# Attention feeding a top-1 mixture of experts: the threshold's float16 parts subtracted by TensorE in PSUM, and the first expert's low halves subtracted from a PSUM copy

## The chip, the cores and the metric

One Trainium2 chip, one core of it, one launch. The metric is device microseconds of the core, the median of a few executions. The engines of the core are named as the profile names them: PE (TensorE matmuls) and PEld (its weight loads), DVE (VectorE), ACT (ScalarE), POOL (GpSimd), SP (SyncE, which here only issues transfers).

## The reference

Thresholded attention over 8 batches of 8 heads (sequence 576, head dimension 64), then a mixture of 8 experts in which each token goes to one expert:

```python
scores = scale * np.matmul(q, k.transpose(0, 1, 3, 2))
thresh = np.max(scores, axis=-1, keepdims=True) - tau
scores = np.where(scores >= thresh, scores, -1000000000.0)
attn = np.exp(scores - np.max(scores, axis=-1, keepdims=True))
attn = attn / (np.sum(attn, axis=-1, keepdims=True) + 1e-09)
x = np.matmul(attn, v)                  # laid out as 4608 tokens of 512
logits = x @ w_gate                     # 8 experts, expert_idx = argmax
h = np.maximum(xe @ w1[e], 0.0)         # 512 -> 1024, tokens of expert e
out[mask] = gate_w[mask, None] * (h @ w2[e])
```

All matmuls run in float16 with a number split in a high and a low half, `hi = f16(x)` and `lo = f16(x - hi)`, so that three products stand for one in float32.

## The kernel before, in words

The attention works on 32 pairs of heads. A pair takes 11 **steps**; the loop over steps writes out, for each step k, one `st_unit` of pair n (transposed scores less the threshold, exponential, mask), one `s_unit` of a later pair, 21 steps ahead, (plain scores, of which DVE takes the row maxima, L324 and L319), and then the products with v of an earlier pair (`av_piece`, L422 to L424). Side work is posted to a step with `plan(k, ...)` or `after(k, ...)` and comes in one of three places: FRONT, MID (after the two units' matmuls) or END (after the mask, ahead of the products with v). `chain(1, [...])` posts its items half a step apart, beginning at the MID of the next step. A planner then orders each engine's instructions: it takes the written order as priority and works with durations of its own, so an instruction may move past others on its engine. `tc.keep_in_program_order` forbids that one instruction moves ahead of what was written before it on its engine.

**The threshold.** `parts(n)` takes the minimum of the negated row maxima (L331), turns the 9 columns with a TensorE transpose into a bank of PSUM (tile `pst`, L335, out of the pool `ps_m`, which has one bank for `pst`, `lg`, `rk` and `pc`), and cuts `x + thr` into three float16 parts (tile `ptT`): ACT makes the first (L340), DVE forms the rest in PSUM (L341), ACT rounds it (L342), DVE subtracts once more (L343). Three small DMAs on SP then put the parts in rows 64 to 66 of the tile `CQ` (L348), where the `st_unit` of the same pair reads them through L361, about seven steps later.

**Low halves.** `low_part` (L244, L245) is the way in which q, k and v get theirs: TensorE multiplies the high half by a float16 identity into a bank of `ps_sc` (6 banks, shared with the score tiles), and DVE subtracts that bank from the scaled input. The experts' weights get theirs in `split_w`: ACT makes the high half of a 128 x 1024 chunk (L730), and one DVE instruction subtracts it, both tensors in SBUF (L731).

**The first expert's weights.** While the last two pairs run, the eight chunks of expert 0 are loaded through two buffers (`wf`, 512 KB each, L717 on SP) and split, one chunk a step from step 318 on (`WS0` = 6 and `WSD` = 1 from step 312); the load of chunk i + 2 is written at the step of split i and must wait until split i has read its buffer. The experts' matmuls (L819, L852) begin to be mixed in about step 342 and fill TensorE from 640 us to the end. The other experts' weights go through eight buffers.

Of the kernel before, what the change touches and what calls it, by code (L numbers as in the profile page):

```python
# [9 lines left out]
F16 = mybir.dt.float16  # L10
# [3 lines left out]
AF = mybir.ActivationFunctionType  # L14
ALU = mybir.AluOpType
AX = mybir.AxisListType

P = 128
# [21 lines left out]
SW = 64.0  # L40
# [2 lines left out]
CAP = NTOK  # L43

TUNE = dict(
    lead=10, cast=2, sl=8, ll=15, sp0=3, sps=0, lv=-16, sv0=-6, sv1=2, av=2, g=4, l=3, d=4, g5=4, l5=3, d5=2, g6=1, l6=2, d6=2, g7=1, l7=1, d7=1, off=2, off5=1, off6=11, lg=4, lg7=13, km=16, rate=15, dh=1, do=3, ws0=6, wsd=1, w1d=5, plv=1, xv=3, so=0, sto=0, ord=0, sc=6, fa=3, fd=4, wa1=-70, wa2=-86, wl1=-28, wl2=-6, avb=1, route=1, ranks=7, pp=8, ew=4, maskat=0, w1a=-40, w1b=3,
)


# [1 line left out]
def kernel(  # L51
# [9 lines left out]
    nc = tc.nc  # L61

    cpool = ctx.enter_context(tc.tile_pool(name="cpool", bufs=1))
# [7 lines left out]
    ew = ctx.enter_context(tc.tile_pool(name="ew", bufs=4))  # L71
# [8 lines left out]
    pp = apool.enter_context(tc.tile_pool(name="pp", bufs=8))  # L80


    ident = cpool.tile([P, P], F32, name="ident")
    make_identity(nc, ident)
    ident_h = cpool.tile([P, P], F16, name="ident_h")
    nc.gpsimd.tensor_copy(ident_h, ident)
    ones = cpool.tile([P, P], F16, name="ones")
    nc.gpsimd.memset(ones, 1.0)
    before = cpool.tile([P, P], F16, name="before")
# [3 lines left out]
    thr = cpool.tile([P, 1], F32, name="thr")  # L93
# [75 lines left out]
    FRONT, MID, END = range(3)  # L169
# [3 lines left out]
    def plan(k, f, where=END):  # L173
        if urgent[0]:
            f = hurry(f)
        assert (k, where) >= (now[0], slot[0])
        acts.setdefault(k, ([], [], []))[where].append(f)
# [11 lines left out]
    def after(k, f, where=END):  # L189
        plan(now[0] + k, f, where)  # L190

    def chain(k, fs, at_once=False):

        if at_once:
            for f in fs:
                after(k, f, END)
            return
        for i, f in enumerate(fs):
            i += slot[0] > FRONT and k == 0
            after(k + i // 2, f, END if i % 2 else MID)  # L200
# [37 lines left out]
    def low_part(x, hi, lo, scale, nm):  # L238

        sc = ps_sc.tile([P, 512], F32, tag="sc", name=f"hi_{nm}")  # L240
        y = sc[:, 0:hi.shape[1]] if len(hi.shape) == 2 else (
            sc[:, 0:hi.shape[1] * hi.shape[2]].rearrange("p (t d) -> p t d", t=hi.shape[1])
        )
        nc.tensor.matmul(y, ident_h, hi, start=True, stop=True)  # L244
        nc.vector.scalar_tensor_tensor(lo, x, scale, y, ALU.mult, ALU.subtract)  # L245
# [80 lines left out]
    def parts(n):  # L326


        nm = st[n]["nm"]
        r = small.tile([P, 9], F32, tag="r", name=f"r_{n}")  # L330
        nc.vector.tensor_reduce(r, nm.rearrange("p a t -> p t a"), axis=AX.X, op=ALU.min)  # L331

        def turn():
            ps = ps_m.tile([P, 512], F32, tag="m", name=f"pst_{n}")
            nc.tensor.transpose(ps[0:9, 0:P], r, ident)  # L335
            x, y = ps[0:9, 0:P], ps[0:9, P:2 * P]
            t = small.tile([9, 3, P], F16, tag="ptT", name=f"ptT_{n}", bufs=1)
            v, a = nc.vector, nc.scalar
            chain(1, [
                lambda: a.activation(t[:, 0], x, AF.Identity, bias=thr[0:9]),  # L340
                lambda: v.scalar_tensor_tensor(y, x, thr[0:9], t[:, 0], ALU.add, ALU.subtract),  # L341
                lambda: a.copy(t[:, 1], y),  # L342
                lambda: (v.tensor_tensor(t[:, 2], y, t[:, 1], ALU.subtract), rows(t)),  # L343
            ])

        def rows(t):
            for p in range(3):
                nc.sync.dma_start(  # L348
                    st[n]["CQ"][64 + p:65 + p].rearrange("p (t c) -> p t c", t=9), t[:, p]
                )  # L350

        after(1, turn)
# [372 lines left out]
    def split_w(e, w, c):  # L725
        wf = wq.pop((e, w, c))

        o = (wb1, wb2)[w][0 if e == "x" else e % 2][:, c].rearrange("p (a h d) -> p a h d", a=w + 1, h=2)
        x = wf.rearrange("p (a d) -> p a d", a=w + 1)
        nc.scalar.activation(o[:, :, 0], x, AF.Copy, scale=SW)  # L730
        nc.vector.scalar_tensor_tensor(o[:, :, 1], x, SW, o[:, :, 0], ALU.mult, ALU.subtract)  # L731

    def late(m):
# [258 lines left out]
    for i in range(8):  # L992
        plan(k + WS0 + WSD * i, lambda i=i: split_w(*wseq[i]))
        if i + 2 < 8:
            plan(k + WS0 + WSD * i, lambda i=i: load_w(*wseq[i + 2]))
# [31 lines left out]
    for e in range(1, E + NL):  # L1027
        for w in range(2):
            for c in range(4):
                i = 4 * w + c  # L1030
# [26 lines left out]
    def weights(j):  # L1057
        turn[0] = j + 1
        split_done.add(wseq[j])
        split_w(*wseq[j])  # L1060
        if j + 8 < len(wseq):
            load_w(*wseq[j + 8])
# [4 lines left out]
    if True:  # L1067
# [9 lines left out]
        while busy:  # L1077
# [3 lines left out]
            for z in (("st", "s"), ("s", "st"))[TUNE["ord"]]:  # L1081
                n, t = divmod(k + (NSTEP + LEAD if z == "s" else 0), NSTEP)
# [11 lines left out]
            n, t = divmod(k - TUNE["av"], NSTEP)  # L1094
# [25 lines left out]
    with tc.For_i(NL, total) as m:  # L1120
        idx = small.tile([P, 2], I32, tag="idx", name="idx_x", bufs=1)
        nc.vector.tensor_copy(idx.unsqueeze(1), T["row"][:, ds(m, 1)])
        bad = small.tile([P, 2], I32, tag="badx", name="bad_x", bufs=1)
        nc.vector.tensor_copy(bad.unsqueeze(1), T["bad"][:, ds(m, 1)])
        regs["x"] = nc.sync.value_load(T["esi"][0:1, ds(m, 1)], min_val=0, max_val=E - 1)
        for w in range(2):
            for c in range(4):
                load_w("x", w, c)
                split_w("x", w, c)
        slots["x"] = idx, bad, 0  # L1130
        fetch("x")
        for g in gemm1, gemm2:
            for _ in g(("x",)):
                chunk[0] += 1
            while mo:
                for _, f in mo.pop(min(mo)):
                    f()
# [52 lines left out]
```

## Time and profile before

| | before |
|---|---|
| median of 3 runs | 1040.5 us (1040.37 to 1044.72) |
| the profiled execution's own time | 1042.02 us |
| its span, first to last instruction | 1040.3 us |
| mean granted TensorE clock | 0.976 of full speed |
| PE, DVE, ACT, POOL busy | 92%, 69%, 63%, 53% of the span |

The busy shares are means over two unlike halves: the attention, to about 600 us, in which PE, DVE, ACT and POOL are all busy most of the time, and the experts, from 640 us, in which PE alone is. A busy PE is an upper bound of its work, since its pipelined matmuls overlap: two matmuls that start 0.22 us apart each last 0.38 us. In a list of instructions the time from one start to the next is what one costs its engine.

### The profile page before, as it was taken

The page shows a single profiled execution, that of the slowest core. Times are in us where ns is not written, and L with a number is a line of the kernel's source. Part 1 is how long each engine was busy: PE and PEld are TensorE (multiplying, and loading weights), DVE is VectorE, ACT ScalarE, POOL GpSimd, SP SyncE. Part 2 cuts the span into 40 slices and gives each one's busy share as a digit, 9 for nine tenths or more (in the row PEclk, how much of TensorE's full clock was granted, in tenths as well). Part 3 has the DMA queues.
Part 4 walks back from the last instruction along what each step waited for, and adds up shares of the span by engine and source line. Part 5 has one row for each costly group of instructions (what it writes and reads, how often), then busy time and mean ns, then how long its engine had stood idle before and what let it go on. Part 6 is the DMA issues. An engine that isn't in the chain of part 4 may idle for free.

```text
span 1040.3 us, 28272 instructions
## 1 busy us (share of the span) xinstructions
PE 958.2 (92%) x11336; PEld 622.9 (60%) x11336; DVE 719.1 (69%) x1443; ACT 653.1 (63%) x1098; POOL 556.3 (53%) x460
## 2 busy tenths in 40 slices
PE   2799998999898998998996689999999999999996
PEld 1365655566464665564663476767766676667683
DVE  6999998899797997997998964664332433423650
ACT  2588998888787987987977773524342433433641
POOL 3266887976977967968867773153221222122121
PEclk9999999899999999999998898999999999999998
DMA  6534554754465645546534536989746746556720
GB/s 185 140 92 110 138 131 116 164 122 116 132 156 144 134 102 155 139 105 180 127 87 134 140 84 214 310 266 236 231 142 172 232 132 178 170 156 217 225 82 25
DMA packets 142562, 159.16 MB, mean 153 GB/s; under 512 B 96345, under 2 KB 112731, under 8 KB 142428
## 3 DMA queue, kind: packets, MB, share of 16 engines
q1 hardware_dynamic: 126796, 100.35, 37.7%
q10 hardware_dynamic: 6480, 27.53, 8.9%
q0 software_dynamic: 9152, 29.45, 8.7%
q8 instruction: 90, 1.47, 0.6%
q14 instruction: 44, 0.36, 0.1%
HBM read 90.24 MB, written 19.44 MB: 105 GB/s over the span
## 4 chain that ended last, share of the span: by engine, by line
PE 50%; DVE 7%; issue 6%; DMA 4%; ACT 3%; POOL 1%; another core or an unknown queue 1%; POOLq 0%; ACTq 0%; DVEq 0%; SPq 0%
PE h L819 16%; PE y L852 14%; PE st L360 3%; PE s L312 3%; PE s L314 3%; PE st L361 3%; PE av L422 2%; DMA out_dram<-o,gt 2%; DVE wb L731 2%; PE av L423 2%; PE av L424 2%; DVE e L380 2%; DVE nm L324 1%; DMA wf<-in_w_dram 1%
## 5 line engine op out<-in xcount | busy, mean ns | idle before, releaser
L386 POOL TENSOR_TENSOR pl<-e,ph 128x1024 f16<-128x1024 f32 x158 | 336.8, 2142 | 144.2 <-ACT ph L385 103.2
L377 ACT ACTIVATE e<-st,ntau 128x512 f32<-128x512 f32 (+1 forms) x352 | 223.1, 653 | 65.5 <-PE st L361 36.2
L324 DVE TENSOR_REDUCE nm<-s 128x1 f32<-128x512 f32 x320 | 200.4, 633 | 39.9 <-PE s L314 26.0
L380 DVE SCALAR_TENSOR_TENSOR e<-st,e 128x512 f32<-128x512 f32 (+1 forms) x352 | 219.8, 635 | 5.4 <-ACT e L377 4.6
L852 PE MATMUL y<-wb,hl 128*128 128x512 f16 (+1 forms) x1056 | 203.6, 362 | 1.1 <-issue 0.7
L819 PEld LDWEIGHTS <-wb 128*128 128x128 f16 x2304 | 190.4, 99 | 23.3 <-issue 4.9
L819 PE MATMUL h<-xTm,wb 128*128 128x256 f16 (+2 forms) x2112 | 198.0, 255 | 3.1 <-issue 3.1
L422 PE MATMUL av<-vop,ph 128*128 128x65 f16 (+1 forms) x1536 | 186.3, 195 | 4.7 <-issue 2.5
L424 PE MATMUL av<-vop,ph 128*128 128x64 f16 (+1 forms) x1536 | 185.7, 196 | 2.3 <-issue 2.3
L423 PE MATMUL av<-vop,pl 128*128 128x65 f16 (+1 forms) x1536 | 184.8, 194 | 3.2 <-issue 2.9
L385 ACT CAST ph<-e 128x1024 f16<-128x1024 f32 x160 | 166.8, 1043 | 18.6 <-DVE e L380 18.3
L422 PEld LDWEIGHTS <-ph 128*128 128x128 f16 (+1 forms) x1536 | 148.8, 101 | 31.5 <-issue 11.9
L423 PEld LDWEIGHTS <-pl 128*128 128x128 f16 (+1 forms) x1536 | 148.6, 100 | 29.1 <-issue 12.3
L312 PE MATMUL s<-QK 128*128 128x512 f16 (+3 forms) x640 | 141.4, 299 | 24.7 <-DMA QK<-lo 17.3
L424 PEld LDWEIGHTS <-ph 128*128 128x128 f16 (+1 forms) x1536 | 148.7, 100 | 24.7 <-issue 11.5
L731 DVE SCALAR_TENSOR_TENSOR wb<-wf,wb 128x1024 f16<-128x1024 f32 x96 | 125.2, 1341 | 49.1 <-ACT wb L730 45.7
L852 PEld LDWEIGHTS <-hl 128*128 128x128 f16 (+1 forms) x1056 | 94.5, 100 | 101.3 <-issue 6.3
L360 PE MATMUL st<-QK 128*128 128x512 f16 (+3 forms) x640 | 142.4, 298 | 8.8 <-DVE e L380 5.3
L361 PE MATMUL st<-CQ,ck 128*128 128x512 f16 (+3 forms) x640 | 139.7, 293 | 0.7 <-DMA CQ<-hi 0.4
L314 PE MATMUL s<-ck,CQ 128*128 128x512 f16 (+3 forms) x640 | 137.8, 292 | 1.2 <-DMA CQ<-hi 1.2
L864 POOL DMA_INDIRECT out_dram<-o,gt x40 | 44.4, 1111 | 143.9 <-ACT o L863 127.1
L807 ACT ACTIVATE hl<-h 128x512 f16<-128x512 f32 (+1 forms) x80 | 45.8, 573 | 113.6 <-PE h L819 106.7
(182 smaller groups left out, 1092.8 us busy)
## 6 DMA issues: line engine op xcount, KB each, us to landing
wf<-in_w_dram SPq DMA_DIRECT2D x96, 512.0 KB
qkf<-in_qk_dram ACTq DMA_DIRECT2D x30, 576.0 KB
vf<-in_v_dram ACTq DMA_DIRECT2D x15, 640.0 KB
QK<-hi SPq DMA_DIRECT2D x64, 144.0 KB
QK<-hi SPq DMA_DIRECT2D x64, 72.0 KB
QK<-lo SPq DMA_DIRECT2D x64, 72.0 KB
ck<-lo SPq DMA_DIRECT2D x64, 72.0 KB
CQ<-hi SPq DMA_DIRECT2D x64, 64.0 KB
```

What stands on the lines that cost most here:

```text
L312: nc.tensor.matmul(sc[rows, oc], d["QA"][a][:, cols], d["KB"][a][:, CH[c]], start=True, stop=False)
L324: nc.vector.tensor_reduce(o, sc[:, 0:width(t)], axis=AX.X, op=ALU.max, negate=True)
L360: nc.tensor.matmul(sc[rows, oc], d["KB"][a][:, cols], d["QA"][a][:, CH[c]], start=True, stop=False)
L361: nc.tensor.matmul(sc[rows, oc], d["CK"][a][:, cols], d["CQ"][:, q], start=False, stop=True)
L377: nc.scalar.activation(pf, sc, AF.Exp, bias=ntau, scale=0.125 / SS)
L380: nc.vector.scalar_tensor_tensor(pf, sc, 0.0, pf, ALU.is_ge, ALU.mult)
L386: (nc.vector if (n, t) in PLV else nc.gpsimd).tensor_tensor(l, pd, h, ALU.subtract)
L422: nc.tensor.matmul(av, h, vop[:, tv, 0:W], start=i in (0, NT) and m == 0, stop=False)
L423: nc.tensor.matmul(av, l, vop[:, tv, 0:W], start=False, stop=False)
L424: nc.tensor.matmul(av[:, 0:D], h, vop[:, tv, W:W + D], start=False, stop=last)
L819: nc.tensor.matmul(o, Wt[:, c, wh, f], x, start=c == 0 and z == 0, stop=c == 3 and z == 2,)
L852: nc.tensor.matmul(o, h[:, hh], Wt[:, f, wh, c], start=f == 0 and z == 0, stop=f == 7 and z == 2)
```

## The change

Three edits. (1) In `parts`, the two DVE instructions go. ACT makes all three parts with the same instruction, `part(p)`, and between them TensorE subtracts the part just made from the bank, `less(p)`: a matmul of a 9 x 9 matrix of minus one on the diagonal by the 9 x 128 part, added to what the bank holds. The chain has five items in place of four, so the third part and its DMAs are posted half a step later. (2) In `split_w`, for expert 0 alone, the low half is made by `low_part` in two pieces of 512 columns, posted two steps after the high half, one at MID and one at END; the high half is kept in program order on ACT. (3) The splits of expert 0, and the loads that are written with them, are two steps apart (`wsd=2`). One small DVE instruction at the start makes the 9 x 9 matrix.

```diff
-    ... ws0=6, wsd=1, w1d=5 ...
+    ... ws0=6, wsd=2, w1d=5 ...
+    minus = cpool.tile([9, 9], F16, name="minus")
+    nc.vector.tensor_scalar(minus, ident[0:9, 0:9], -1.0, None, ALU.mult)
@@ parts: turn()
-            nc.tensor.transpose(ps[0:9, 0:P], r, ident)
-            x, y = ps[0:9, 0:P], ps[0:9, P:2 * P]
+            nc.tensor.matmul(ps[0:9, 0:P], r, ident, start=True, stop=True, is_transpose=True)
+            x = ps[0:9, 0:P]
             t = small.tile([9, 3, P], F16, tag="ptT", name=f"ptT_{n}", bufs=1)
+            def part(p):
+                nc.scalar.activation(t[:, p], x, AF.Identity, bias=thr[0:9])
+            def less(p):
+                nc.tensor.matmul(x, minus, t[:, p], start=False, stop=True, skip_group_check=True)
             chain(1, [
-                lambda: a.activation(t[:, 0], x, AF.Identity, bias=thr[0:9]),
-                lambda: v.scalar_tensor_tensor(y, x, thr[0:9], t[:, 0], ALU.add, ALU.subtract),
-                lambda: a.copy(t[:, 1], y),
-                lambda: (v.tensor_tensor(t[:, 2], y, t[:, 1], ALU.subtract), rows(t)),
+                lambda: part(0), lambda: less(0), lambda: part(1), lambda: less(1), lambda: (part(2), rows(t)),
             ])
@@ split_w
-        nc.scalar.activation(o[:, :, 0], x, AF.Copy, scale=SW)
+        hi = nc.scalar.activation(o[:, :, 0], x, AF.Copy, scale=SW)
+        if e == 0:
+            tc.keep_in_program_order(hi)
+            for i in range(2):
+                t = slice(512 * i, 512 * i + 512)
+                y = (x[:, i], o[:, i, 0], o[:, i, 1]) if w else (x[:, 0, t], o[:, 0, 0, t], o[:, 0, 1, t])
+                after(2, lambda y=y, i=i: low_part(*y, SW, f"w{w}_{c}_{i}"), END if i else MID)
+            return
         nc.vector.scalar_tensor_tensor(o[:, :, 1], x, SW, o[:, :, 0], ALU.mult, ALU.subtract)
```

## Rows read from the trace of the kernel before

**Rows 1.** Busy time by stretch (from and to in us of the span, its length, then busy us and count of instructions for PE, PEld, DVE, ACT, POOL; then the granted clock, the DMA engines' share, GB/s): the steady attention, the stretch of the eight splits, what follows it, and the experts.

```profile
60.00:540.00 480.00, 457.37 (x6693) 281.06 (x6691) 427.69 (x909) 406.01 (x733) 371.93 (x238) 0.98 0.52 129
556.00:598.00 42.00, 26.57 (x337) 16.58 (x334) 41.19 (x58) 29.47 (x50) 32.14 (x20) 0.84 0.47 114
617.00:640.00 23.00, 18.39 (x273) 15.29 (x270) 4.93 (x23) 2.84 (x11) 9.65 (x11) 0.82 0.41 138
640.00:1000.00 360.00, 357.67 (x2891) 248.88 (x2890) 160.51 (x259) 149.26 (x197) 89.48 (x113) 1.00 0.70 207
```

**Rows 2.** The splits' DVE instruction alone: its busy time in 556 to 598 us (the same columns, DVE alone), and its least, median and longest duration in ns with the starts of the first and last; then all 96 chunks of the whole span (count | busy us, mean ns | idle before).

```profile
556.00:598.00 42.00, 20.69 (x8) 0.84 0.47 114
L731 DVE SCALAR_TENSOR_TENSOR wb<-wf,wb x8: 1209/2493/5526, 556.5 to 594.3; 128x1024 f16<-128x1024 f32 x8
L731 DVE SCALAR_TENSOR_TENSOR wb<-wf,wb 128x1024 f16<-128x1024 f32 x96 | 125.2, 1341 | 49.1 <-ACT wb L730 45.7
```

**Rows 3.** DVE in order of time around the first two splits (start, us, instruction, count, and in brackets the idle time before it and what ended it).

```profile
555.84 0.69 DVE L324 TENSOR_REDUCE nm<-s 128x1 f32<-128x512 f32 x1 [4.09 <-PE s L314]
556.45 5.53 DVE L731 SCALAR_TENSOR_TENSOR wb<-wf,wb 128x1024 f16<-128x1024 f32 x1
561.90 0.68 DVE L380 SCALAR_TENSOR_TENSOR e<-st,e 128x512 f32<-128x512 f32 x1
562.50 0.68 DVE L324 TENSOR_REDUCE nm<-s 128x1 f32<-128x512 f32 x1
563.10 1.21 DVE L731 SCALAR_TENSOR_TENSOR wb<-wf,wb 128x1024 f16<-128x1024 f32 x1
564.23 0.68 DVE L324 TENSOR_REDUCE nm<-s 128x1 f32<-128x512 f32 x1
```

**Rows 4.** POOL and PE in order of time beside that first split (the same columns).

```profile
556.69 4.20 POOL L386 TENSOR_TENSOR pl<-e,ph 128x1024 f16<-128x1024 f32 x2
562.63 0.38 PE L312 MATMUL s<-QK 128*128 128x512 f16 x1 [4.30 <-DVE e L380]
564.96 0.58 PE L312 MATMUL s<-QK 128*128 128x512 f16 x1 [1.41 <-DVE nm L324]
```

**Rows 5.** The chain of waits that ended last, 552 to 600 us, by line (cut by the view), and two of its pieces: the last chunk's load and ACT's half of the split behind it.

```profile
by line: DVE wb L731 39.5%; DVE e L380 10.2%; DMA wf<-in_w_dram 8.1%; issue 7.2%; DVE nm L324 6.6%; PE s L314 4.2%; DVE s_e L934 3.2%; PE st L360 2.8%; PE s L312 2.6%; ACT wb L730 2.2%; DVE has L615 2.2%; PE st L361 2.1%; DVE vop L245 1.6%;
589.28 3.90 DMA wf<-in_w_dram
593.25 1.06 ACT wb L730
```

**Rows 6.** The DVE instruction of `low_part` for q and k, over the whole span (least, median, longest ns).

```profile
L245 DVE SCALAR_TENSOR_TENSOR lo<-qkf,hi x93: 530/544/555, 18.6 to 538.4; 128x384 f16<-128x384 f32 x93
```

**Rows 7.** The chain of waits that ended last, 280 to 540 us, by line (shares of the stretch, cut by the view).

```profile
by line: PE s L312 10.8%; PE st L360 10.4%; PE s L314 9.1%; PE st L361 8.5%; PE av L422 7.8%; PE av L424 6.7%; PE av L423 6.6%; issue 4.9%; DVE nm L324 4.6%; DVE e L380 4.4%; ACT e L377 2.8%; ACT ph L385 2.6%; PE hi L244 2.1%; DVE lo L245 2
```

**Rows 8.** One pair's threshold on DVE and on ACT, in order of time, with the instruction that follows each.

```profile
284.89 0.35 DVE L341 SCALAR_TENSOR_TENSOR pst<-pst,thr,ptT 9x128 f32<-9x128 f32 x1
285.16 1.00 DVE L245 SCALAR_TENSOR_TENSOR lo<-qkf,hi 128x384 f16<-128x384 f32 x2
287.18 0.28 DVE L343 TENSOR_TENSOR ptT<-pst,ptT 9x128 f16<-9x128 f32 x1 [0.40 <-ACT ptT L342]
287.39 0.67 DVE L324 TENSOR_REDUCE nm<-s 128x1 f32<-128x512 f32 x1
284.51 0.34 ACT L340 ACTIVATE ptT<-pst,thr 9x128 f16<-9x128 f32 x1
284.76 0.73 ACT L276 ACTIVATE vop<-vf 128x640 f16<-128x640 f32 x1
286.90 0.25 ACT L342 CAST ptT<-pst 9x128 f16<-9x128 f32 x1
287.06 1.13 ACT L472 CAST R<-xn 128x512 f16<-128x512 f32 x2
```

**Rows 9.** PE in order of time: full-width matmuls of 512 and the threshold's transpose at 299 us, and a change between the half-array form (128*64) and the full form (128*128) at 545 us.

```profile
299.46 0.38 PE L312 MATMUL s<-QK 128*128 128x512 f16 x1
299.68 0.38 PE L314 MATMUL s<-ck,CQ 128*128 128x512 f16 x1
299.90 0.27 PE L335 MATMUL pst<-ident,r 128*9 128x128 f32 x1
300.00 0.19 PE L423 MATMUL av<-vop,pl 128*128 128x65 f16 x1
...
545.15 0.19 PE L424 MATMUL av<-vop,ph 128*64 128x64 f16 x1
545.18 0.20 PE L422 MATMUL av<-vop,ph 128*64 128x65 f16 x1
545.31 0.39 PE L360 MATMUL st<-QK 128*128 128x512 f16 x1
```

**Rows 10.** Waits of the whole span (who waited for whom: us in total, times, longest): the copies of `low_part` on PE, and the threshold's own waits.

```profile
PE hi_v L244 <- ACT vop L276: 7.1, 4, 3.8
PE hi L244 <- ACT hi L230: 3.6, 6, 0.9
PE hi_v L244 <- ACT ptT L340: 3.0, 1, 3.0
DVE pst L341 <- ACT ptT L340: 4.7, 4, 2.2
DVE ptT L343 <- ACT ptT L342: 0.7, 2, 0.4
ACT ptT L342 <- DVE pst L341: 5.3, 7, 2.4
```

**Rows 11.** The minimum that opens each pair's threshold (32 of them, first and last start), and ACT's exponential (count | busy us, mean ns | idle before).

```profile
L331 DVE TENSOR_REDUCE r<-nm x32: 152/164/175, 29.1 to 583.5; 128x9 f32<-128x18 f32 x32
L377 ACT ACTIVATE e<-st,ntau 128x512 f32<-128x512 f32 (+1 forms) x352 | 223.1, 653 | 65.5 <-PE st L361 36.2
```

**Rows 12.** SP's queue in order of time: loads of `wf` (three in one entry: from the first's issue to the last's), the threshold's rows, and the transposes of the expert input.

```profile
544.90 17.43 SPq L717 DMA_DIRECT2D wf<-in_w_dram  x3
562.43 0.78 SPq L348 DMA_DIRECT2D CQ<-ptT  x1
...
589.70 1.24 SPq L480 DMA_TRANSPOSE xTg<-R  x1
```

More of the change, by code (lines that the diff above doesn't have):

```diff
@@ L45 @@
 TUNE = dict(
-    lead=10, cast=2, sl=8, ll=15, sp0=3, sps=0, lv=-16, sv0=-6, sv1=2, av=2, g=4, l=3, d=4, g5=4, l5=3, d5=2, g6=1, l6=2, d6=2, g7=1, l7=1, d7=1, off=2, off5=1, off6=11, lg=4, lg7=13, km=16, rate=15, dh=1, do=3, ws0=6, wsd=1, w1d=5, plv=1, xv=3, so=0, sto=0, ord=0, sc=6, fa=3, fd=4, wa1=-70, wa2=-86, wl1=-28, wl2=-6, avb=1, route=1, ranks=7, pp=8, ew=4, maskat=0, w1a=-40, w1b=3,
+    lead=10, cast=2, sl=8, ll=15, sp0=3, sps=0, lv=-16, sv0=-6, sv1=2, av=2, g=4, l=3, d=4, g5=4, l5=3, d5=2, g6=1, l6=2, d6=2, g7=1, l7=1, d7=1, off=2, off5=1, off6=11, lg=4, lg7=13, km=16, rate=15, dh=1, do=3, ws0=6, wsd=2, w1d=5, plv=1, xv=3, so=0, sto=0, ord=0, sc=6, fa=3, fd=4, wa1=-70, wa2=-86, wl1=-28, wl2=-6, avb=1, route=1, ranks=7, pp=8, ew=4, maskat=0, w1a=-40, w1b=3,
 )
@@ L334, in turn @@
             ps = ps_m.tile([P, 512], F32, tag="m", name=f"pst_{n}")
-            nc.tensor.transpose(ps[0:9, 0:P], r, ident)
-            x, y = ps[0:9, 0:P], ps[0:9, P:2 * P]
+            nc.tensor.matmul(ps[0:9, 0:P], r, ident, start=True, stop=True, is_transpose=True)
+            x = ps[0:9, 0:P]
             t = small.tile([9, 3, P], F16, tag="ptT", name=f"ptT_{n}", bufs=1)
-            v, a = nc.vector, nc.scalar
+            def part(p):
+                nc.scalar.activation(t[:, p], x, AF.Identity, bias=thr[0:9])
+            def less(p):
+                nc.tensor.matmul(x, minus, t[:, p], start=False, stop=True, skip_group_check=True)
             chain(1, [
-                lambda: a.activation(t[:, 0], x, AF.Identity, bias=thr[0:9]),
-                lambda: v.scalar_tensor_tensor(y, x, thr[0:9], t[:, 0], ALU.add, ALU.subtract),
-                lambda: a.copy(t[:, 1], y),
-                lambda: (v.tensor_tensor(t[:, 2], y, t[:, 1], ALU.subtract), rows(t)),
+                lambda: part(0), lambda: less(0), lambda: part(1), lambda: less(1), lambda: (part(2), rows(t)),
             ])
```

## The prediction, made before the changed kernel was run

> **What bounds the kernel now.** I began with the busy time by stretch, since a mean over the span mixes attention and experts. From 640 to 1000 us PE is busy 357.67 of 360 us [rows 1]: nothing in the change touches that half, except that it begins earlier or later. So the whole question is how long it takes to get there. From 60 to 540 us PE is busy 457.37 of 480 us, DVE 427.69 (89%), ACT 406.01 (85%) [rows 1]. PE leads, but only just. The chain of waits says how often it sets the pace: between 280 and 540 us its listed PE lines sum to 62% of the stretch, the DVE lines to about 11%, the ACT lines to about 5% [rows 7]. I use these shares as weights: a microsecond of work taken off an engine, or put on it, moves the end by that share. The stretch from 556 to 598 us is another matter. There PE is busy only 26.57 of 42 us, and DVE 41.19, which is 98% [rows 1]; half of that, 20.69 us, are the eight splits [rows 2], and L731 alone is 39.5% of the chain from 552 to 600 us [rows 5]. Here DVE is the bound.
>
> **Why those splits are dear.** They are not slow by nature: one took 1.21 us, and the next DVE instruction starts 1.13 us after it [rows 3]. But they reach 5.53 us, with a median of 2.49, where all 96 have a mean of 1.34 [rows 2]. The 5.53 us one starts at 556.45; POOL starts two subtractions at 556.69 that last 4.20 us, to 560.89, and the split ends 1.1 us after them, about its own undisturbed length [rows 3, 4]. So it stood still while POOL ran. PE then sat idle 4.30 us until the mask behind the split was done, and its next matmuls, at 564.96, took 0.58 in place of 0.38 us: the granted clock of 556 to 598 us is 0.84, against 0.98 in the steady part [rows 1, 4].
>
> The Trainium skill ("SBUF — State Buffer", Who interferes with whom) states that a VectorE instruction with two SBUF inputs contends with a GpSimd instruction that reads SBUF, and that one with at most one does not; the rows above agree with the first half.
>
> **Edit 2, the low halves from PSUM.** Does a subtraction from PSUM escape? The same instruction of `low_part`, 384 wide, lasted 530 to 555 ns in all 93 cases [rows 6], in a stretch where POOL is busy 371.93 of 480 us [rows 1]. A wait would show as a long tail, and there is none. So I price the 16 new pieces of 512 as the mask of that size, which reads PSUM and SBUF: 0.60 us from its start to the next [rows 3], 9.6 us in all. DVE loses 20.69 and gains 9.6: **minus 11.1 us**. In the same stretch it also loses two pairs' threshold work, 2 x 0.48 = 1.0 us (below). The load left is then 41.19 - 20.69 + 9.6 - 1.0 = 29.1 us on DVE, and on ACT 29.47 plus two pairs' 0.34 = 30.2 us. PE gets 16 copies of 512 columns at 0.22 us [rows 9], 3.5 us, inside its 15.4 us of idle. What does a stretch with a 30.2 us engine last? At 98%, as DVE runs there now, 30.8 us; at the 89% of DVE in the steady part, 33.9 us [rows 1]. That is 11.2 to 8.1 us less than 42, and I take the middle, **-9.6 us**.
>
> **Edit 3, two steps apart, and the loads.** Each buffer goes round so: a load, 3.90 us from its issue at 589.28 to the start of ACT's split; ACT 1.06 us [rows 5]; two steps until the low half; two pieces, 1.2 us. A step is (583.5 - 29.1) / 31 / 11 = 1.63 us [rows 11]. Together 9.4 us for two chunks, three rounds, after a first of 5.5 us without its load: 33.8 us. That is as long as the upper end above, so the loads are just covered and I add nothing; if SP issues one late, ACT waits in order at the pinned high half, with exponentials of 0.65 us [rows 11] behind it, and PE waits for those. SP did hold things up: three loads span 544.90 to 562.33, since the third waits for the first split, and the threshold's rows stand behind it [rows 12]. With short splits that hold shrinks.
>
> **Edit 1, the threshold.** Per pair DVE loses 0.27 + 0.21 = 0.48 us, counted from each start to the next; ACT goes from 0.25 + 0.16 to 3 x 0.25, plus 0.34 us [rows 8]. Over 32 pairs DVE has 15.4 us less and ACT 10.9 more; weighted by 11% and 5% this is -1.7 and +0.5 us. If the weights are wrong, both ends are full: DVE's 15.4 us gained, ACT's 10.9 lost.
>
> PE gets 64 small float16 matmuls, and before shows none of that shape. By columns, 128 of 512 at 0.22 us [rows 9] is 0.055 us. The transpose, in float32 and with nine columns of weights, takes 0.10 us to the next start. Changing between the full and the half-array form costs 0.13 us where 0.03 is normal [rows 9], so a piece of 9 x 9 may pay 0.10 twice, 0.255 us. Ends: 3.5 and 16.3 us. I take 0.08, between the column price and the transpose, because entering and leaving the nine-column transpose shows no such gap: 5.1 us, times 62% is +3.2 us (ends +2.2, +10.1).
>
> The Trainium skill ("TensorEngine Tiling (Array Packing)", Key Properties) says that switching the tiling mode drains TensorE, and it speaks against this edit. The 0.13 us row agrees for the half array; whether nine rows of weights are a mode of their own no row here shows. By the rule the term would be +10.1 us, by the transpose's row +4.0.
>
> Then waiting: PE works in order and each `less` needs ACT's part posted half a step before it. The nearest case are the 157 copies that wait for ACT's high halves: 7.1 + 3.6 + 3.0 = 13.7 us of PE idle [rows 10], 0.087 us each. For 64: 5.6 us, times 62% is +3.5 (below it zero, if the planner places them late enough). Gone are the waits of DVE for ACT, 4.7 + 0.7, and of ACT for DVE, 5.3 us [rows 10]: times their weights -0.9. The DMAs of the rows leave half a step, 0.8 us, later, with seven steps (11 us) until L361 reads them: nothing; without that cover it would be 0.8 us a pair. The same holds for the one bank of `ps_m`, kept half a step longer.
>
> The start's 9 x 9 instruction is one small DVE piece among set-up work: nothing, at most some tenths.
>
> **Sum.** -9.6 for the stretch; +3.2 +3.5 -0.9 -1.7 +0.5 = +4.6 for the threshold: -5.0 us. The profiled execution took 1042.0 us, so 1037.0; the median of the runs lies 1.5 us lower, so **1035.5 us**. About 0.5%, 5.2 us, is what a measurement can tell from no change.
>
> **Rivals.**
> *TensorE waits for ScalarE (slower).* If each `less` finds ACT behind, every pair stalls PE twice. ACT is 85% busy, and an exponential of 0.65 [rows 11] and a part of 0.25 us ahead are 0.90 us; half of that as a stall, 0.45 us, is 64 x 0.45 x 62% = 17.9 us. With the other terms (-9.6 + 3.2 - 0.9 - 1.7 + 0.5 = -8.5) the sum is +9.4: 1050. It turns slower by more than 5.2 us from 0.35 us a stall on. For it: the planner's durations are its own, and one copy waited 3.0 us behind L340 [rows 10]. Against it: the copies' mean of 0.087.
> *The drains of TensorE.* At 0.255 us a piece the sum is -5.0 + 6.9 = +1.9: 1042. Against it the transpose's row.
> *The loads become the bound.* The stretch keeps its 42 us if a round takes (42 - 5.5) / 3 = 12.2 us, 2.8 more than worked out, for instance behind transposes of 1.24 us on SP [rows 12]. Then +4.6: 1045.
> *DVE really paces the attention.* With its 15.4 us worth half, not 11%, the sum is -5.0 - 6.0: 1029.
> *The change does not free DVE.* If pieces from PSUM waited for POOL as well, the stretch stays: 1045; rows 6 speak against it.
>
> **Chances.** The forecast's mechanism 0.50 (ends: -11.2 with the waits at zero and PE at +2.2 gives -11; -8.1 with more waiting gives 0), DVE pacing 0.10, drains 0.15, TensorE waiting 0.15, loads 0.08, no relief 0.02. Splitting the first at -5.2 (0.30 faster, 0.20 same), the second to faster, drains 0.11 same and 0.04 slower, waiting 0.04 and 0.11, loads and no relief 0.05 and 0.05: faster 0.40, same 0.40, slower 0.20. The range 1027 to 1046 leaves out the better half of DVE pacing and most of the waiting, about 0.17; the likeliest case alone spans 1029 to 1041.
>
> **What would show it.** Right: sixteen L245 pieces near 0.68 us with no tail in the splits' stretch, DVE there below 90%, PE's 4.3 us idle gone, the clock near 0.98, the experts' full stretch beginning some 5 us earlier; L335's bank with 64 matmuls, each under 0.1 us to the next start, PE's idle for ACT there under 6 us. Wrong: PE idle behind `less` of 15 us or more; ACT idle for `wf` at the pinned high halves; the steady pair longer than 17.9 us; or the gained time lost again at 617 to 640 us, where PE is idle 4.6 of 23 us for other reasons [rows 1].

## The result, and the profile after

The changed kernel took **1048.2 us** (median, 1047.0 to 1052.3) against 1041.4 us for the kernel before in the same measurement: a ratio of 1.0065, 95% interval 1.0042 to 1.0089. It is slower, by 6.8 us; 1035.5 us had been predicted, with a range of 1027 to 1046. The profiled execution took 1048.0 us, its span 1046.2 at a mean clock of 0.977.

What answers to [rows 1], in the changed kernel (the same columns):

```profile
60.00:540.00 480.00, 455.82 (x6600) 278.76 (x6600) 412.46 (x840) 410.68 (x748) 367.12 (x236) 0.99 0.52 128
556.00:598.00 42.00, 34.48 (x446) 20.56 (x446) 33.11 (x70) 33.19 (x59) 32.46 (x26) 0.88 0.65 160
617.00:640.00 23.00, 22.15 (x358) 18.84 (x357) 10.02 (x18) 9.16 (x20) 9.92 (x10) 0.94 0.78 194
640.00:1000.00 360.00, 351.90 (x2798) 243.84 (x2796) 154.12 (x248) 144.73 (x189) 87.18 (x109) 0.99 0.67 201
```

The splits' stretch looks as foreseen: DVE fell from 41.19 to 33.11 us, PE rose from 26.57 to 34.48. The steady part has 15.2 us less on DVE, 4.7 more on ACT. But PE did 93 instructions fewer there, and from 640 to 1000 us, where the kernel before left PE idle for only 2.3 us, PE is busy 5.8 us less.

What answers to [rows 2, 6, 9, 10]: the pieces of the splits on DVE (least, median, longest ns); the 64 `less` on PE (busy us, mean ns | idle before); and who waited for whom (us in total, times, longest; the two load lines are for 540 to 610 us, the splits, and for 640 to 700 us).

```profile
L247 DVE SCALAR_TENSOR_TENSOR wb<-wf,hi_w x16: 669/676/689, 561.8 to 597.1; 128x512 f16<-128x512 f32 x16
L346 PE MATMUL pst<-ptT,minus 9*9 9x128 f16 x64 | 14.1, 220 | 12.1 <-ACT ptT L343 6.7 <-issue 3.0 <-ACT hi L232 2.3
```

```profile
PE pst L346 <- ACT ptT L343: 6.7, 5, 4.7
ACT ptT L343 <- PE pst L346: 4.6, 8, 1.4
ACT wb L736 <- DMA wf<-in_w_dram: 1.8, 3, 1.3
ACT wb L736 <- DMA wf<-in_w_dram: 7.0, 2, 5.8
```

Sixteen pieces within 20 ns of each other, while POOL was busy 32.46 of the 42 us: here a subtraction with one input in PSUM did not wait for POOL. In front of its 64 `less` PE sat idle for 12.1 us, 6.7 of them for ACT's part by name. ACT waited 1.8 us for loads at the high halves of the eight splits; its longer waits for loads lie behind 640 us, at other experts' weights.

One `less` among the products with v, in order of time:

```profile
287.90 0.19 PE L428 MATMUL av<-vop,ph 128*128 128x65 f16 x1
287.93 0.19 PE L429 MATMUL av<-vop,pl 128*128 128x65 f16 x1
288.05 0.22 PE L346 MATMUL pst<-ptT,minus 9*9 9x128 f16 x1
288.20 0.20 PE L430 MATMUL av<-vop,ph 128*128 128x64 f16 x1
288.24 0.20 PE L428 MATMUL av<-vop,ph 128*128 128x65 f16 x1
```

The starts are the reading: 0.03 to 0.04 us from one product to the next, but 0.12 into the `less` and 0.15 out of it. From the product before it to the product behind it there are 0.27 us where 0.03 was due, so a `less` costs **0.24 us net**. The median of these distances is 0.276 us, over all `less` that stand alone. The prediction had 0.08.

### The profile page after: what moved, and what is told of

Same layout as the page of the kernel before. It is cut to its first block, busy times and chain, and to the rows that moved or that the text cites. A ratio compares the mean times of both kernels' runs of the same rounds, so it can differ in the third digit from the quotient of the medians.

```text
span 1046.2 us, 28360 instructions
## 1 busy us (share of the span) xinstructions
PE 970.9 (93%) x11416; PEld 628.3 (60%) x11416; DVE 701.7 (67%) x1388; ACT 667.3 (64%) x1130; POOL 553.2 (53%) x460
## 4 chain that ended last, share of the span: by engine, by line
PE 77%; DVE 6%; issue 6%; DMA 5%; ACT 3%; SPq 2%; another core or an unknown queue 1%; POOL 0%; POOLq 0%; ACTq 0%; DVEq 0%
PE h L832 17%; PE y L865 14%; PE st L366 7%; PE s L314 7%; PE st L367 6%; PE s L316 6%; PE av L428 5%; PE av L429 5%; PE av L430 5%; DMA out_dram<-o,gt 3%; DVE nm L326 2%; DVE e L386 2%; PE hi L246 2%; PE hi_v L246 1%; DMA wf<-in_w_dram 1%
## 5 line engine op out<-in xcount | busy, mean ns | idle before, releaser
L386 DVE SCALAR_TENSOR_TENSOR e<-st,e 128x512 f32<-128x512 f32 (+1 forms) x352 | 223.2, 644 | 5.2 <-ACT e L383 4.8
L832 PE MATMUL h<-xTm,wb 128*128 128x256 f16 (+2 forms) x2112 | 200.3, 256 | 5.9 <-issue 5.0
L430 PEld LDWEIGHTS <-ph 128*128 128x128 f16 (+1 forms) x1536 | 148.0, 100 | 22.4 <-issue 11.1
L366 PE MATMUL st<-QK 128*128 128x512 f16 (+3 forms) x640 | 139.8, 296 | 4.3 <-DVE nm L326 3.7
L744 DVE SCALAR_TENSOR_TENSOR wb<-wf,wb 128x1024 f16<-128x1024 f32 x88 | 105.1, 1233 | 54.5 <-ACT wb L736 52.3
```

Source lines behind the costliest of these rows:

```text
L366: nc.tensor.matmul(sc[rows, oc], d["KB"][a][:, cols], d["QA"][a][:, CH[c]], start=True, stop=False)
L386: nc.vector.scalar_tensor_tensor(pf, sc, 0.0, pf, ALU.is_ge, ALU.mult)
L430: nc.tensor.matmul(av[:, 0:D], h, vop[:, tv, W:W + D], start=False, stop=last)
L832: nc.tensor.matmul(o, Wt[:, c, wh, f], x, start=c == 0 and z == 0, stop=c == 3 and z == 2,)
```

## The experiments

The groups ran on four chips (the second and the fourth on the same one), and times are compared within a group or as a ratio to the kernel before there (1046.4, 1021.4, 1043.4, 1026.2 and 1044.1 us in the five groups, in the order below). In brackets stands the 95% interval.

**One part at a time.** Edit 1 alone (`thr_only`), edits 2 and 3 (`low_ws2`), edit 2 (`low_ws1`), edit 3 (`ws2_only`):

```diff
 thr_only: the kernel before, with the new turn() and the matrix minus
 low_ws2:  the kernel before, with low_part in split_w for e == 0, and wsd=2
 low_ws1:  the same with wsd=1
 ws2_only: the kernel before, with wsd=2
```

> The kernel before with edit 1 alone (the threshold's parts subtracted by TensorE). Theory G (give-back: the threshold costs nothing per pair, the splits' gain is real and lost again behind 640 us): the minima that open the pairs 1 to 25 lie within 1 us of before, the stall of 5.5 us at the first split is still there, and the end is 1041 to 1047 us, the upper part only if the single late spot between pairs 25 and 26 (+5.7 us in the changed kernel) comes with this edit. Rival T (the threshold costs TensorE per pair): each pair 0.2 us longer, 1047 us or more with the loss spread evenly.

> The kernel before with edits 2 and 3 alone (first expert's low halves from a PSUM copy, splits two steps apart). Theory G: the splits' stretch is 8 to 11 us shorter than before, TensorE is 8 to 11 us ahead at 640 us, and most of it is lost by 720 us, where the DMA engines are full: 1036 to 1042 us. Rival T (all the loss is the threshold's): the gain stays to the end, 1029 to 1034 us.

> The kernel before with edit 2 alone, splits one step apart as before. Theory G: no stalled splits, and the same give-back behind 640 us: 1036 to 1042 us. If the loads set the splits' pace, the stretch is no shorter than with two steps; if the two steps hold it up, it is 2 to 5 us shorter, with ScalarE waiting for the loads at the high halves kept in order.

> The kernel before with edit 3 alone, the splits from SBUF two steps apart. All theories: the eight splits still meet GpSimd, with some of them over 2 us; 1038 to 1046 us. If the spacing were what spoils the start of the experts, it would be 1046 us or more here.

Measured: `thr_only` 1.0041 (1.0012 to 1.0070), `low_ws2` **0.9909** (0.9878 to 0.9939), `low_ws1` 1.0001 (0.9973 to 1.0028), `ws2_only` 1.0006 (0.9978 to 1.0034). So the splits give their 9.5 us, but only as both edits together; the threshold costs 4.3 us alone; and the two sum to -5.2 us, where +6.8 was measured. They do not add up. Neither theory had this: the splits' gain stayed to the end, as T said, and the threshold alone cost as little as G said.

With one step apart ACT waits for the splits' loads more than with two (540 to 610 us, `low_ws1` and then `low_ws2`):

```profile
ACT wb L730 <- DMA wf<-in_w_dram: 6.1, 4, 3.1
ACT wb L730 <- DMA wf<-in_w_dram: 3.5, 1, 3.5
```

That is 2.6 us more, where `low_ws1` lacks 9.5; what took the rest was not tested.

In the traces one place stood out. From the minimum of pair 25 (L331, in the new code L333) to that of pair 26 the kernel before takes 21.95 us, `low_ws2` 21.96, but `thr_only` 27.73 and the changed kernel 27.66. There GpSimd issues four indirect transfers (the puts of L566), and ACT's first part waits for the transpose's result (ACT, PE and POOL of the changed kernel, in order of time; of the four puts, the first and the last):

```profile
469.97 1.03 ACT L391 CAST ph<-e 128x1024 f16<-128x1024 f32 x1
476.65 0.36 ACT L343 ACTIVATE ptT<-pst,thr 9x128 f16<-9x128 f32 x1 [5.65 <-remote]
```

```profile
471.85 0.28 PE L337 MATMUL pst<-ident,r 128*9 128x128 f32 x1
477.06 0.26 PE L346 MATMUL pst<-ptT,minus 9*9 9x128 f16 x1 [4.65 <-ACT ptT L343]
```

```profile
470.71 1.01 POOL L566 DMA_INDIRECT xs<-R,posi  x1 [1.31 <-ACT R L559]
474.55 0.96 POOL L566 DMA_INDIRECT xs<-R,posi  x1 [0.30 <-issue]
```

The transpose began at 471.85 and is listed with 0.28 us; ACT could read its result only at 476.6, after the last put, with `less` stuck behind it in order. A second suspect lay at 691 to 700 us, where the gathers are issued: PE went from one short matmul to the next in 0.7 us, its share fell to 1.41 of 4 us and the granted clock behind it to 0.50.

**Are these two places the loss?** The changed kernel again; with the former threshold at pair 25 alone (`old25`); with the gathers meant to start some 4 us later (`after_late`), and so for `low_ws1`, which had the second place too:

```diff
 old25:
-        after(1, turn)
+        after(1, turn_before if n == 25 else turn)
 after_late, low_ws1_late (table_first):
+        for _ in range(20 if nm == "2" else 0):
+            nc.vector.tensor_scalar(rk, rk, 0.0, None, ALU.add)
```

> The changed kernel once more, beside the other three of this group. Both theories: 1.003 to 1.009 of the kernel before; minimum of pair 25 to minimum of pair 26 27.7 us; TensorE between 688 and 700 us idle for about 5 us with the clock at half behind it.

> The changed kernel, but pair 25 alone makes its threshold's parts as the kernel before did (two subtractions on VectorE). Theory 'late completions': the new threshold code costs its time at the one pair whose turn falls into the GpSimd stretch of four indirect puts (470 to 476 us), because it has three trips TensorE to ScalarE there instead of one and TensorE's completions arrive 2 to 5 us late. Then pair 25 to pair 26 takes 22 us (21.5 to 22.5) instead of 27.7, and the end comes 3 to 6 us sooner than the changed kernel's unless the stretch of 640 to 715 us gives it back. Rival 'a cost per pair or the planner's order': 25 to 26 stays near 27 us and the end within 2 us of the changed kernel's.

> The changed kernel with twenty additions of zero on VectorE (some 4 us of it) ahead of the row table that the gathers at 687 us wait for, so that this stretch of GpSimd gathers starts about 4 us later; the results are the same. Theory 'the gathers meet gemm1': TensorE's short matmuls (h, 0.06 us apart) run dry while GpSimd issues indirect transfers back to back, its long ones (y, 0.21 us apart) do not; 4 us later the gathers meet y for most of their time, TensorE's idle time in 684 to 704 us falls from 6 us to under 3, its clock stays at full, and the end comes 3 to 7 us sooner though VectorE does more. Rival 'the gathers are needed sooner': the end comes 2 to 4 us later. Rival 'no phase matters': within 1 us.

> The kernel before with the low halves of the splits by the copied rounding (one step apart), and the same twenty additions of zero. Without them it showed TensorE idle 6.2 us and its clock at half between 680 and 704 us, and 1.000 of the kernel before. Theory 'the gathers meet gemm1': the idle time falls under 3 us, 0.993 to 0.997. Rival 'the gathers are needed sooner': 1.002 to 1.005.

Measured: 1.0071 (1.0039 to 1.0103), 1.0066 (1.0038 to 1.0093), 1.0053 (1.0022 to 1.0084), 0.9998 (0.9966 to 1.0031). On this chip the places did not show: under GpSimd's bursts of transfers no result of TensorE came over 1 us late. In the unaltered changed kernel ACT waits 1.16 us for the transpose, not 5.65,

```profile
471.69 0.36 ACT L343 ACTIVATE ptT<-pst,thr 9x128 f16<-9x128 f32 x1 [1.16 <-PE pst L337]
```

pair 25 takes 20.92 us, beside the gathers TensorE stands still once, 1.70 us for a transfer's data, and the kernel is still 0.7% slower than before. So neither place is needed for a loss, and the theory that the late spots are the loss fell for this chip. Whether they add to it where results do come late, these runs cannot tell; `after_late` is not distinguishable from the unaltered kernel.

**All four corners on one chip.** The kernel before, each part, both:

> The kernel before, for a profile beside the next three on one chip. Ratio 0.998 to 1.002. Both theories: the last score matmul to the 144th gemm2 matmul 88 us (85 to 91).

> The kernel before with the low halves by the copied rounding, two steps apart, and the former threshold code. Theory 'the two edits do not add up': 0.988 to 0.995 again, and the last score matmul to the 144th gemm2 matmul about 80 us. Rival 'one chip's late completions': where GpSimd's bursts delay nothing, the gain is gone and the ratio is 0.997 to 1.001.

> The kernel before with the new threshold code alone. Theory 'the two edits do not add up': 1.002 to 1.007, pair 25 to pair 26 up to 27 us where completions come late, 21 to 22 us where they do not, and in both cases TensorE waiting over 6 us for the transposes of the last batch's rows between 620 and 670 us. Rival 'one chip's late completions': 0.999 to 1.002 where pair 25 to 26 takes 21 to 22 us.

> The changed kernel beside the three. Theory 'the two edits do not add up': 1.004 to 1.010, more than the sum of the two edits alone by 0.8 to 1.4%; the difference against the second kernel of this group builds up between the last score matmul and the 144th gemm2 matmul (12 us or more of it). Rival 'a cost of the threshold code spread over the pairs': the difference against the second kernel is there by pair 30 already, over 8 us.

Measured: 1.0003 (0.9976 to 1.0031), **0.9909** (0.9872 to 0.9945), 1.0061 (1.0029 to 1.0092), 1.0039 (1.0010 to 1.0067). The interplay, what both together lose beyond the sum of the parts, is there again at 0.7%; with the three intervals taken as independent that is 0.1 to 1.3%.

Pair 25 is late on this chip too, in both kernels with the new threshold: 27.07 us in the threshold alone and 27.82 in both, against 21.94 before and 21.92 in the splits alone (the minima of the kernel before, then of the threshold alone):

```profile
465.03 0.17 DVE L331 TENSOR_REDUCE r<-nm 128x9 f32<-128x18 f32 x1
486.97 0.16 DVE L331 TENSOR_REDUCE r<-nm 128x9 f32<-128x18 f32 x1
465.51 0.18 DVE L333 TENSOR_REDUCE r<-nm 128x9 f32<-128x18 f32 x1
492.58 0.16 DVE L333 TENSOR_REDUCE r<-nm 128x9 f32<-128x18 f32 x1
```

So the threshold alone is 0.5 us behind the kernel before at pair 25 and 5.6 at pair 26, and its last matmul comes 5.7 us later. Both together are 2.8 us behind the splits alone at pair 25, 8.7 at pair 26, 9.1 at pair 30 and 14.5 at the last matmul; from the last score matmul to the 144th of gemm2 they take 91.5 us, the splits alone 78.4. Of the two marks set for the last kernel, the theory's (12 us or more behind the last score matmul) and the rival's (over 8 us by pair 30) were thus both met; its ratio, 1.0039, and the interplay came out just below what the theory had. A kernel with the former threshold at pair 25 alone was never run on such a chip (both such runs met the other one), so the late spot at pair 25 stays an untested rival for what the threshold costs here.

The rows of PE (length, busy us, granted clock) for 28 to 440, 556 to 640 and 640 to 720 us, first of the kernel before, then the splits alone, the threshold alone, both:

```profile
28.00:440.00 412.00, 387.91 (x5443) 0.97 0.52 129
556.00:640.00 84.00, 65.88 (x988) 0.84 0.41 109
640.00:720.00 80.00, 77.01 (x852) 0.98 1.00 285
```

```profile
28.00:440.00 412.00, 388.95 (x5466) 0.97 0.52 130
556.00:640.00 84.00, 75.18 (x1101) 0.94 0.55 151
640.00:720.00 80.00, 73.63 (x793) 0.98 0.97 267
```

```profile
28.00:440.00 412.00, 391.34 (x5463) 0.98 0.53 129
556.00:640.00 84.00, 70.59 (x1133) 0.90 0.54 154
640.00:720.00 80.00, 69.75 (x770) 0.94 0.99 264
```

```profile
28.00:440.00 412.00, 391.74 (x5441) 0.98 0.52 128
556.00:640.00 84.00, 71.29 (x1157) 0.96 0.64 145
640.00:720.00 80.00, 72.71 (x768) 0.96 0.95 265
```

They suggest an account. From 28 us to the last gemm2 matmul, time is by definition TensorE's work (busy time times granted clock) plus its idle time plus what a lowered clock loses. Summed over windows of 2 us, on these four profiled executions:

| us of TensorE | before | splits | threshold | both |
|---|---|---|---|---|
| 28 us to the last matmul | 1001.6 | 994.4 | 1007.3 | 1008.9 |
| work | 927.0 | 932.2 | 937.3 | 943.8 |
| idle and clock, from 28 to 440 us | 35.7 | 33.6 | 28.6 | 29.3 |
| the same, 440 to 560 us | 8.0 | 8.8 | 9.2 | 10.0 |
| the same, 560 to 640 us | 26.6 | 11.8 | 19.0 | 15.5 |
| the same, 640 to 730 us | 4.3 | 8.1 | 13.3 | 10.1 |

The work nearly adds up: 5.2 and 10.3 alone, 16.8 together. The relief does not. In 560 to 640 us the splits alone remove 14.8 us of lost time, the threshold alone 7.6, both together 11.1. An explanation is that they free the same idle time, and it can be freed once; it does not say why both together free 3.7 us less than the splits alone. From 640 to 730 us time is lost again, in the threshold alone most, where the logits wait for transposes of the last batch (7.2 us there, 2.2 in both). The late pair 25 hardly shows in 440 to 560 us (8.0 against 9.2), since TensorE had other work meanwhile; how much of it reaches the end is open.

**Is it TensorE's own time?** To `low_ws2` small matmuls are added that nobody reads, two or four per pair; the former threshold code stays. Beside them pair 25's exception once more, and the splits three steps apart:

```diff
 low_idle2 (low_idle4: range(2)); the lines between are left out:
+            def idle():
+                for _ in range(1):
+                    nc.tensor.matmul(ps[0:9, 2 * P:3 * P], minus, ones[0:9], start=True, stop=True)
-                lambda: v.scalar_tensor_tensor(y, x, thr[0:9], t[:, 0], ALU.add, ALU.subtract),
+                lambda: (v.scalar_tensor_tensor(y, x, thr[0:9], t[:, 0], ALU.add, ALU.subtract), idle()),
-                lambda: (v.tensor_tensor(t[:, 2], y, t[:, 1], ALU.subtract), rows(t)),
+                lambda: (v.tensor_tensor(t[:, 2], y, t[:, 1], ALU.subtract), rows(t), idle()),
 low_ws3: wsd=3
```

> The kernel before with the low halves by the copied rounding, two steps apart (0.991), and the former threshold code, to which two matmuls of 9x9 by 128 columns per pair are added that nothing reads, at the steps where the new code has its own: 64 more on TensorE, no wait and nothing more on another engine. Theory 'TensorE's own time': a matmul of this shape delays the next one by 0.24 us net, so 64 of them cost 15 us of TensorE, and since TensorE is the bound most of it reaches the end: 0.998 to 1.005. Rival 'the trips between TensorE and ScalarE': nothing waits for these, so 0.990 to 0.994.

> The same with four such matmuls per pair, 128 in all. Theory 'TensorE's own time': twice the loss of the former against 0.991, so 1.005 to 1.018. Rival 'the trips': 0.990 to 0.996.

> The changed kernel with the former threshold code at pair 25 alone, on a chip where completions come late under GpSimd's bursts (if it is one). Theory 'TensorE's own time': the 5.7 us at pair 25 vanish (25 to 26 in 22 us) but the end moves little, 0.999 to 1.006 of the kernel before. Rival 'the late spot is the loss': 0.995 to 0.999.

> The low halves by the copied rounding, the splits three steps apart instead of two, the former threshold code. Both theories: 0.988 to 0.995; it shows whether the distance of the splits still matters.

Measured: 1.0217 (1.0173 to 1.0260), 1.0226 (1.0185 to 1.0266), 1.0057 (1.0027 to 1.0087), 1.0072 (1.0042 to 1.0103). The first is far more than I had allowed, and twice as many matmuls cost nearly nothing more. The trace of `low_idle4` says why the second pair is free:

```profile
293.40 0.19 PE L428 MATMUL av<-vop,ph 128*128 128x65 f16 x1
293.52 0.27 PE L343 MATMUL pst<-ones,minus 9*9 9x128 f16 x2
293.73 0.20 PE L429 MATMUL av<-vop,pl 128*128 128x65 f16 x1
```

Two in a row (they start at 293.52 and 293.58) need 0.33 us from neighbour to neighbour, one needs 0.27. The second costs 0.06, about its column price; the rest, 0.18 us, is paid once for going to the 9 x 9 weights and back. `old25_again` met the chip of the second group again, where pair 25 is not late, and adds nothing. `low_ws3` missed: on this chip three steps apart lose 0.7%; no run of two steps alone stands beside it, so whether the splits gain anything on this chip is not known.

**The same matmuls against the kernel without them, on one chip:**

> The low halves by the copied rounding, two steps apart, the former threshold code, beside the next one. Theory 'the splits' gain holds on every chip': 0.988 to 0.995. Rival 'it depends on the chip' (three steps apart gave 1.007 on the chip of the last group): 0.998 to 1.008 where completions do not come late under GpSimd's bursts.

> The former with 64 matmuls of 9x9 by 128 columns that nothing reads. Theory 'TensorE's own time': 13 to 16 us of TensorE's work more than the former, and 10 to 20 us longer. Rival 'the trips': within 3 us of the former.

Measured: **0.9897** (0.9870 to 0.9924) and 1.0236 (1.0204 to 1.0267), 1033.7 and 1069.6 us: 35.9 us for 64 matmuls without a purpose, where 10 to 20 had been expected. The account takes it apart: work 932.2 to 946.9, +14.7 us, or 0.23 each; idle time +13.2; clock +7.4. And the "no wait" of the expectation was wrong, for they stood in TensorE's order behind VectorE's subtraction, whose tile they share:

```profile
PE pst L343 <- DVE pst L347: 15.8, 7, 5.1
```

```profile
L343 PE MATMUL pst<-ones,minus 9*9 9x128 f16 x64 | 14.3, 224 | 17.7 <-DVE pst L347 15.8 <-DVE ptT L349 1.9
```

So the price in TensorE's work is shown twice, by the starts and by the account; it is less than half of the 35.9 us. (For the threshold's own 64 the account gives less, 10.3 us or 0.16 each; why is not known.) The rest came with waits in TensorE's queue, and these runs do not separate how much a wait-free version would cost.

## Why the prediction was wrong

**The sum: the step that failed.** "-9.6 for the stretch; +3.2 +3.5 -0.9 -1.7 +0.5 = +4.6 for the threshold: -5.0 us" adds the two edits as if each were made on the kernel before. Alone, each came out near its forecast: edits 2 and 3 at -9.5 us, edit 1 at +4.3 us (+6.4 on the chip of the four corners). Their sum, -5.2 us, is the forecast. Together they gave +6.8 us, 12 more than the parts, and 7 more (interval 1 to 13) on the one chip where all four kernels ran. The weights of [rows 7] take each edit alone; they cannot see that both relieve the same stretch. In 560 to 640 us the reliefs of 14.8 and 7.6 us became 11.1. The last line of the prediction named the danger, "the gained time lost again", but at 617 to 640 us, and as a sign only, with no term in the sum.

That this sharing explains all of the 7 to 12 us is not shown. It rests on one profiled execution of each kernel on one chip. The other set, from more than one chip (the first traces of the kernel before and the changed one, and the first group), gives 12.3, 9.9 and 12.2 us for the same stretch, which fits a relief that can be had once. Why the combination loses as much as it does stays open.

**Edit 1, the price of a `less`: a term mis-sized.** "I take 0.08, between the column price and the transpose, because entering and leaving the nine-column transpose shows no such gap." The upper end, 0.255 us, was nearly right: 0.24 measured, about 15.5 us for 64. Its weight of 62% makes 9.6 us of it where the sum had 3.2; the account shows 10.3 us more work in the threshold alone. The transpose was the wrong neighbour, and the half-array change [rows 9] the right one, and I gave that case a chance of 0.15. What makes the difference is not shown: the 9 x 9 weights have few rows and few columns (9\*9), the transpose has 128 rows, nine columns and float32 (128\*9), and the half array, with 128 rows and 64 columns, pays 0.13 us as well.

This term does not explain the miss. With the right price, 6.4 us more, the forecast for edit 1 alone would have been +11.0, and +4.3 to +6.4 was measured. That edit 1 alone came out near +4.6 is luck: the price was too low, and the relief was too low as well. It had -1.7 and -0.9 us in the sum, where TensorE's lost time fell by 7.1 us in 28 to 440 us and by 7.6 in 560 to 640.

The Trainium skill ("TensorEngine Tiling (Array Packing)", Key Properties) has a change of tiling mode drain TensorE. The trace agrees, with 0.12 us on the way in and 0.15 us on the way out of a `less`; that such a tile is a mode of its own is read from these gaps.

**Edit 1, the waits: too small, and of another shape.** 5.6 us of PE idle were forecast. Measured were 6.7 for ACT's part by name, and 12.1 in all in front of the 64. They come in few waits, one of 4.65 us; it is no rate per instruction. DVE's relief in 60 to 540 us was 15.2 us (15.4 forecast for the whole), ACT's load 4.7 more (10.9 forecast).

**Edits 2 and 3 and the splits' stretch: right.** The pieces took 669 to 689 ns without a tail, DVE fell below 90% (33.11 of 42 us, 79%), PE's share rose as said. -9.6 us were forecast; edits 2 and 3 without edit 1 gave 0.9909, 0.9909 and 0.9897 on three chips, 9.5 to 10.8 us. The agreement is partly luck: the sum had no term for the 16 copies on PE outside the stretch's idle time, and the account has 5 us more work, against 12 us less lost time. Edit 3 was read as just covering the loads, and so it came out: at the eight high halves ACT waited 1.8 us for them, and with one step apart, where it waited 6.1, the gain was gone (1.0001).

**The rivals.** The drains were true as a price, but on the prediction's terms they ended at 1042, since the other terms were added as if independent. TensorE waiting for ScalarE at every pair did not happen: by name there were five waits in front of 64 `less`. The loads did not become the bound. A version that beats both kernels came out of it: the changed splits with the former threshold, about 0.99 of the kernel before on each of the three chips it ran on.

## What to carry to other kernels

Where TensorE is the bound, count a small matmul by the starts of its neighbours, not by its columns: here one with 9 x 9 weights among full ones cost 0.24 us, and a second one beside it 0.06, so put such matmuls side by side or leave the work on an engine with slack. When two edits both relieve one stretch, do not add their gains: add the new work in full, and price the second edit on the kernel after the first. Measure the parts alone: here the loser hid a winner. And when a wait is counted as a sign, ask where in the span it lies.

## What the runs showed of the hardware

A semaphore is the counter by which one engine tells another that a result is there. Under GpSimd's bursts of indirect transfers (three or more in a row) TensorE's semaphore rose late in the traces, up to 6.8 us after the modelled end of the matmul that raises it (`ws2_only`). In the changed kernel 35 of the 36 completions that came more than 0.9 us late lie in such bursts, which fill 50 to 60 us of the span; in the kernel before 48 of 51. These counts are upper bounds, since the traces also lack 15 to 20 of the rises. On one chip, where the kernel before took 1021 to 1026 us in place of 1041 to 1046, eight profiles of changed versions show three such completions in all, of 0.9 to 1.0 us. What differs between the chips, and what makes the semaphores late, no run here tells.

In such a burst of the changed kernel TensorE passes from one short matmul to the next in 0.7 us without waiting for any semaphore, and the granted clock behind it was 0.50, the lower of its two levels, 1.2 of 2.4 GHz (PE of the changed kernel by stretch: length, busy us, clock, DMA share, GB/s):

```profile
688.00:692.00 4.00, 3.55 (x56) 1.00 0.66 149
692.00:696.00 4.00, 1.41 (x8) 0.84 1.15 245
696.00:700.00 4.00, 3.52 (x33) 0.50 1.09 243
```
